# An adaLN transformer block on one core: the jump over the fallback program stands ahead of the last output transfers of SyncE and the last operations of VectorE

## The chip, the core and the metric

The kernel runs on one core of a Trainium2 chip. A core has five engines, each with its own instruction stream and its own sequencer: TensorE (PE in the profile, with PEld for its weight loads) multiplies matrices into PSUM, VectorE (DVE) and ScalarE (ACT) work element by element, GpSimd (POOL) does little here, and SyncE (SP) issues DMA transfers. Engines wait for each other through semaphores. The metric is the device time of the whole launch in microseconds (us), lower is better. Times of before and after are medians of several runs.

## The reference

One block with modulation from a condition `c`: six vectors (shift, scale and gate, for the attention and for the feed-forward half) come from `silu(c) @ w_mod`; then

```
h = layernorm(x) * (1 + ca) + sa
x = x + ga * attention(h)        # 32 query heads of 32, one key and value head, S = 2048
h = layernorm(x) * (1 + cb) + sb
x = x + gb * ((silu(h @ w1) * (h @ w3)) @ w2)     # D = 1024, F = 3584
```

All inputs and the output are bf16; `x` is 2048 x 1024. What matters for this case is the last line: for each group of rows, the product with `w2` is multiplied by the gate `gb`, added to `x`, and sent to the output in DRAM.

## The kernel before

The 2048 rows are worked on in 8 blocks of 256 rows (`NB`, `B`). For each block the attention, its output projection, the feed-forward's first half and its second half follow; blocks overlap, so that TensorE has products to do while ScalarE takes exponentials. The program is written as a graph of operations (`Graph.op`), and `Placer` puts them in an order, per engine, from a written list (`ORDER`). Each operation becomes a small function that issues its waits, its instruction and its semaphore update; `Placer.ops[name]` is the list of these functions for one engine. All of them are played through line 22, so line 22 is what the profile shows for nearly every instruction.

**Two programs.** The fast program takes the softmax without subtracting the row maximum. While it runs, VectorE checks that the sums stay in a safe range (`in_range`), and when the last block's sums are through, `verdict` writes one number, `AGAIN`: 0 if all was well. The same kernel holds a second, guarded program, in which the maximum is subtracted. Every engine first plays its whole list of the first program, then waits for the flag, loads `AGAIN` into a register (line 747), and compares and branches (line 748): if the number isn't 0 it plays the second program, otherwise it jumps over it. With the inputs here it is 0, so the second program is never run, but its instructions lie in each engine's stream between the first program and the end of the block. SyncE, after the jump, waits for the transfers of the first program's output (line 756). Line 758 is the end of the block, where the engines drain, meet at a barrier through GpSimd, and finish.

**The end of the first program.** The feed-forward's second half (`ffn2`, `quarter`, `result`) goes through four quarters of 256 output columns for a block. A quarter is 28 matmuls for each of two halves of 128 rows. For a whole quarter VectorE multiplies the 128x512 result by the gate (`HT<-S,GBR` in the profile) and adds it to `x` (`X<-X,HT`). In the last block each quarter is sent out as soon as it is summed, by a transfer of 128 KB on SyncE's queue; the last quarter is handled half by half, with 64 KB each. So the last things on VectorE are: product and sum of the third quarter, product and sum of the first half of the fourth, product and sum of its second half, six operations; and on SyncE the three transfers that belong to them. Each transfer has its own semaphore, for which line 756 waits.

Of the kernel before, what the change touches and what calls it, by code (L numbers as in the profile page):

```python
# [24 lines left out]
class Sess:  # L25
    __slots__ = ("bank", "nodes", "left", "prev", "strict", "allow", "fill")

    def __init__(self, strict=True):
        self.fill = False
        self.allow = ()  # L30
        self.strict = strict
        self.bank = None
        self.nodes = []
        self.left = 0
        self.prev = ()
# [375 lines left out]
class Placer:  # L411
# [6 lines left out]
    FULL = 36.0  # L418
    FETCH = 24.0
    GAP = 0.7  # L420

    def __init__(self, g, banks, later, plan, first=None, order=None):
        self.g = g
# [150 lines left out]
    def commit(self, n, e, k, start):  # L574
# [12 lines left out]
        if e == "pe" and self.warm and self.step == 0 and n.mode == "F":  # L587
            self.keep_warm(start)
        elif e == "pe" and self.warm and self.step and start - before > self.GAP:
            self.keep_on(before, start)  # L590
# [148 lines left out]
    def emit_all(self, second, flag, tile, outs):  # L739
        sem = self.sem  # L740
        last = self.finals()

        def both(eng, name):
            for fn in self.ops[name]:
                fn(eng)
            eng.wait_ge(sem[flag.sem], flag.val)
            again = eng.value_load(tile)
            with eng.If(again != 0):
                for s, v in last.items():
                    if v:  # L750
                        eng.wait_ge(sem[s], v)
                for fn in second.ops[name]:
                    fn(eng)
            if name == "sp":
                for n in outs:
                    eng.wait_ge(sem[n.sem], n.val)

        with self.nc.Block() as block:
            @block.gpsimd
            def _(e):  # L760
                both(e, "pool")

            @block.sync
            def _(e):
                both(e, "sp")

            @block.tensor
            def _(e):
                both(e, "pe")

            @block.scalar
            def _(e):
                both(e, "act")

            @block.vector
            def _(e):
                both(e, "dve")
# [892 lines left out]
```

## Time and profile before

| what | us |
|---|---|
| median of three runs | 1137.85 (1137.28 to 1138.27) |
| profiled execution | 1138.92 |
| its span, first to last instruction | 1137.1 |
| VectorE's last sum ends | 1132.50 |
| SyncE issues the output of the second quarter | 1120.70 |
| SyncE issues the last output | 1132.53 |

The span is what the trace's times refer to: 0 is its start. In the rows, an engine's name with a q behind it (SPq, DVEq, PEldq) means its sequencer, whose waits, loads of registers, branches and DMA issues aren't counted as busy time. A row of a group such as `x1: 505/505/505, 1132.9 to 1132.9` gives the least, median and greatest duration in nanoseconds, and then when the first and the last of the group start. In a timeline's row the first number is the start, the second the duration, and the bracket at its end the idle time ahead of it and what ended that. `q14 instruction` in a list of DMA queues is the fetching of instructions for an engine; `q1` carries the kernel's own transfers.

### The profile page before, as it was taken

The page shows a single profiled execution, that of the slowest core. Times are in us where ns is not written, and L with a number is a line of the kernel's source. Part 1 is how long each engine was busy: PE and PEld are TensorE (multiplying, and loading weights), DVE is VectorE, ACT ScalarE, POOL GpSimd, SP SyncE. Part 2 cuts the span into 40 slices and gives each one's busy share as a digit, 9 for nine tenths or more (in the row PEclk, how much of TensorE's full clock was granted, in tenths as well). Part 3 has the DMA queues.
Part 4 walks back from the last instruction along what each step waited for, and adds up shares of the span by engine and source line. Part 5 has one row for each costly group of instructions (what it writes and reads, how often), then busy time and mean ns, then how long its engine had stood idle before and what let it go on. Part 6 is the DMA issues. An engine that isn't in the chain of part 4 may idle for free.

```text
span 1137.1 us, 37432 instructions
## 1 busy us (share of the span) xinstructions
PE 1102.5 (97%) x16864; PEld 755.2 (66%) x16891; DVE 993.3 (87%) x1634; ACT 1020.4 (90%) x1159; POOL 42.9 (4%) x93
## 2 busy tenths in 40 slices
PE   5999989999899999999999999999999999999998
PEld 5744546766467766777577766776667757777887
DVE  7998999999999989998999889998999899997441
ACT  5999999999999999999999999999999999993110
POOL 5300000000100000000000000000000000000000
PEclk9999999999999999999999999999999999999999
DMA  9321477675656676865696568768587558767983
GB/s 344 107 76 36 146 212 203 191 203 144 174 150 192 183 188 157 240 195 152 122 297 193 151 179 209 223 193 214 149 249 214 161 141 214 214 188 195 260 233 85
DMA packets 381544, 209.73 MB, mean 184 GB/s; under 512 B 17600, under 2 KB 373184, under 8 KB 381376
## 3 DMA queue, kind: packets, MB, share of 16 engines
q1 hardware_dynamic: 380944, 207.11, 66.0%
q8 instruction: 135, 2.21, 0.8%
q14 instruction: 33, 0.27, 0.1%
q10 hardware_dynamic: 432, 0.13, 0.1%
HBM read 199.89 MB, written 4.19 MB: 179 GB/s over the span
## 4 chain that ended last, share of the span: by engine, by line
PE 47%; ACT 41%; DVE 6%; DMA 2%; POOL 1%; issue 1%; SPq 1%; DVEq 0%
ACT U L22 38%; PE PB L22 34%; PE S L22 13%; ACT HT L22 3%; DVE PS L22 2%; DMA W<-in_A_wq_dram 1%; DVE ST L22 1%; DVE HT L22 1%; POOL RS L22 1%; SPq L22 1%; DMA HT<-in_B_w_dram 1%; DVE QT L22 1%; DMA W<-in_B_w_dram 0%; DVE X L22 0%; DVE XNB L22 0%
## 5 line engine op out<-in xcount | busy, mean ns | idle before, releaser
L22 ACT ACTIVATE U<-S 128x1024 bf16<-128x1024 f32 x1024 | 967.0, 1141 | 6.2 <-PE S L22 5.0
L22 DVE TENSOR_TENSOR PS<-U 128x2048 bf16<-128x2048 bf16 x256 | 308.8, 1213 | 9.6 <-ACT U L22 8.1
L22 DVE TENSOR_TENSOR PS<-PS 128x1024 bf16<-128x1024 bf16 (+1 forms) x420 | 284.5, 690 | 4.2
L22 PE MATMUL PB<-QT,W 128*128 128x256 bf16 (+1 forms) x2632 | 223.5, 273 | 0.1
L22 PE MATMUL S<-QT,KT 32*128 32x256 bf16 x4096 | 203.9, 273 | 7.9 <-ACT U L22 5.3
L22 PEld LDWEIGHTS PB<-QT,W 128*128 128x128 bf16 (+1 forms) x2632 | 167.4, 97 | 40.8 <-issue 22.2
L22 PE MATMUL PB<-W2S,HT 128*128 128x256 bf16 x1512 | 189.6, 273 | 0.0
L22 PEld LDWEIGHTS PB<-W2S,HT 128*128 128x128 bf16 x1512 | 137.1, 98 | 41.6 <-issue 22.6
L22 PEld LDWEIGHTS S<-QT,KT 32*128 32x128 bf16 x4096 | 60.8, 92 | 135.4 <-ACT U L22 121.8
L22 PE MATMUL PB<-U,V 128*32 128x256 bf16 x4032 | 126.9, 273 | 0.8 <-ACT U L22 0.8
L22 PE MATMUL PB<-QT,HT 128*128 128x256 bf16 (+1 forms) x1288 | 123.9, 273 | 0.9 <-DVE QT L22 0.6
L22 PEld LDWEIGHTS PB<-U,V 128*32 128x32 bf16 x4032 | 99.4, 96 | 23.2 <-issue 13.5
L22 ACT ACTIVATE HT<-PB 128x512 bf16<-128x512 f32 (+1 forms) x110 | 81.6, 741 | 32.0 <-PE PB L22 31.9
L22 PEld LDWEIGHTS PB<-QT,HT 128*128 128x128 bf16 (+1 forms) x1288 | 90.9, 97 | 23.2 <-issue 11.5
L22 PE MATMUL PB<-HT,W 128*32 128x512 bf16 (+2 forms) x884 | 97.8, 342 | 2.8 <-DVE HT L22 0.9
L22 DVE SCALAR_TENSOR_TENSOR HT<-HT,PB 128x512 bf16<-128x512 bf16 x103 | 70.4, 684 | 12.7 <-ACT HT L22 11.8
L22 PEld LDWEIGHTS PB<-HT,W 128*128 128x128 bf16 (+1 forms) x896 | 50.4, 97 | 33.2 <-issue 11.7
L22 DVE TENSOR_TENSOR HT<-HT,PB 128x512 bf16<-128x512 bf16 x98 | 66.7, 681 | 1.3 <-PE PB L22 0.6
L22 PE MATMUL PB<-WO,QT 128*128 128x512 bf16 (+1 forms) x266 | 54.8, 380 | 1.6 <-issue 1.3
L22 DVE STREAM_TRANSPOSE RB<-PB 128x256 f32<-128x256 f32 x63 | 28.1, 446 | 29.2 <-PE PB L22 28.7
L22 POOL TENSOR_SCALAR RS<-MV 128x1 f32<-128x1 f32 x32 | 13.4, 418 | 1001.0 <-DVE MV L22 994.8
L22 ACT ACTIVATE HT<-S 128x512 bf16<-128x512 f32 (+1 forms) x13 | 9.4, 728 | 36.7 <-PE S L22 36.7
(122 smaller groups left out, 674.8 us busy)
## 6 DMA issues: line engine op xcount, KB each, us to landing
W<-in_B_w_dram SPq DMA_DIRECT2D x150, 512.0 KB, 4.9
W2S<-in_B_w_dram SPq DMA_DIRECT2D x30, 1792.0 KB, 9.3
HT<-in_B_w_dram SPq DMA_DIRECT2D x74, 512.0 KB, 5.0
W2S<-in_w_mod_dram SPq DMA_DIRECT2D x8, 1024.0 KB, 5.7
X<-in_A_x_dram SPq DMA_DIRECT2D x8, 512.0 KB, 6.7
U<-in_w_mod_dram SPq DMA_DIRECT2D x4, 1024.0 KB, 11.6
out_dram<-X SPq DMA_DIRECT2D x7, 512.0 KB, 8.1
W2S<-in_A_x_dram SPq DMA_DIRECT2D x5, 512.0 KB, 11.1
```

Source lines behind the costliest of these rows:

```text
L22: return getattr(e, call[0])(*call[1], **call[2])
```

## The change

`TAIL` names two engines and a number of list entries: 3 for SyncE, 6 for VectorE. These engines now play their list up to that tail, then wait for the flag, load `AGAIN` and branch. In the first `If` (the number isn't 0) the tail comes ahead of the second program, so that the first program is complete there too. A second `If`, on the same register being 0, stands behind it and plays the tail. Then the stream goes on as before: SyncE's waits for the outputs, and the end of the block. The other three engines have a tail of 0 and the same instructions as before. The tail is thus twice in the stream of each of the two engines, and played once.

```diff
+    TAIL = {"sp": 3, "dve": 6}
...
         def both(eng, name):
-            for fn in self.ops[name]:
+            ops = self.ops[name]
+            cut = len(ops) - self.TAIL.get(name, 0)
+            for fn in ops[:cut]:
                 fn(eng)
             eng.wait_ge(sem[flag.sem], flag.val)
             again = eng.value_load(tile)
             with eng.If(again != 0):
+                for fn in ops[cut:]:
+                    fn(eng)
                 for s, v in last.items():
                     if v:
                         eng.wait_ge(sem[s], v)
                 for fn in second.ops[name]:
                     fn(eng)
+            if ops[cut:]:
+                with eng.If(again == 0):
+                    for fn in ops[cut:]:
+                        fn(eng)
             if name == "sp":
                 for n in outs:
                     eng.wait_ge(sem[n.sem], n.val)
```

## The prediction

> **What bounds the kernel now.** I read the page's first lines, then the chain of waits over the last 45 us, because an edit at the end of two queues can touch nothing else, and then, line by line, what the sequencers do behind the last arithmetic. From the page, and from the chain between 1095 and 1140 us (start us, length us, what):
>
> ```profile
> span 1137.1 us, 37432 instructions
> PE 1102.5 (97%) x16864; PEld 755.2 (66%) x16891; DVE 993.3 (87%) x1634; ACT 1020.4 (90%) x1159; POOL 42.9 (4%) x93
> ```
>
> ```profile
> 1125.60 3.06 PE PB L22 x28
> 1128.66 3.07 PE S L22 x28
> 1131.73 0.02 issue
> 1131.75 0.44 DVE HT L22
> 1132.19 0.02 issue
> 1132.21 0.29 DVE X L22
> ```
>
> TensorE sets the pace until 1131.73, and the last operation of VectorE ends at 1132.21 + 0.29 = 1132.50. The span ends at 1137.1. So 4.6 us follow in which no engine computes, and the page counts none of it as busy. The groups of the three lines that run there (value load, branch, and the end of the block with line 756's waits; the times after the commas are first and last start) and SyncE's last issue in the timeline:
>
> ```profile
> L22 DVE TENSOR_SCALAR AGAIN<-S x1: 152/152/152, 1051.9 to 1051.9; 128x1 int32<-128x1 f32 x1
> L747 POOLq TENSOR_LOAD <-AGAIN x1: 498/498/498, 1052.1 to 1052.1; - x1
> L747 DVEq TENSOR_LOAD <-AGAIN x1: 544/544/544, 1132.2 to 1132.2; - x1
> L747 SPq TENSOR_LOAD <-AGAIN x1: 505/505/505, 1132.9 to 1132.9; - x1
> ```
>
> ```profile
> L748 POOLq COMPARE_BRANCH  x1: 45/45/45, 1052.6 to 1052.6; - x1
> L748 ACTq COMPARE_BRANCH  x1: 50/50/50, 1105.8 to 1105.8; - x1
> L748 PEldq COMPARE_BRANCH  x1: 3622/3622/3622, 1130.2 to 1130.2; - x1
> L748 DVEq COMPARE_BRANCH  x1: 72/72/72, 1132.8 to 1132.8; - x1
> L748 SPq COMPARE_BRANCH  x1: 53/53/53, 1133.5 to 1133.5; - x1
> ```
>
> ```profile
> L756 SPq EVENT_SEMAPHORE  x6: 17/28/28, 1136.3 to 1136.7; - x6
> ```
>
> ```profile
> L758 POOLq EVENT_SEMAPHORE  x2: 17/17/17, 1136.9 to 1137.0; - x2
> L758 POOLq DRAIN  x1: 107/107/107, 1053.1 to 1053.1; - x1
> L758 ACTq DRAIN  x1: 80/80/80, 1110.0 to 1110.0; - x1
> L758 PEldq DRAIN  x1: 73/73/73, 1133.8 to 1133.8; - x1
> L758 DVEq DRAIN  x1: 58/58/58, 1135.8 to 1135.8; - x1
> L758 SPq COMPARE_BRANCH  x1: 43/43/43, 1136.7 to 1136.7; - x1
> L758 SPq DRAIN  x1: 13/13/13, 1136.9 to 1136.9; - x1
> ```
>
> ```profile
> 1132.53 0.34 SPq L22 DMA_DIRECT2D out_dram<-X  x1
> ```
>
> Read them by engine. Each branch itself is shown as some 50 ns, but the next instruction of the engine comes much later: SyncE branches at 1133.5 and its first wait runs at 1136.3, **2.8 us** later; VectorE 1132.8 to its drain at 1135.8, 3.0; TensorE 3.6 (here the branch row itself is long); ScalarE 1105.8 to 1110.0, 4.2; GpSimd only 1052.6 to 1053.1, 0.5. GpSimd has by far the shortest program (x93 on the page). Instruction fetches have their own DMA rows, in three windows: around GpSimd's branch (1052 to 1054 us) none shows, around ScalarE's (1105.3 to 1110) one, behind the last arithmetic (1131.5 to 1138) four:
>
> ```profile
> q1 hardware_dynamic: 663, 0.34, 56.1%
> ```
>
> ```profile
> q1 hardware_dynamic: 1899, 0.97, 72.0%
> q14 instruction: 1, 0.01, 1.2%
> ```
>
> ```profile
> q14 instruction: 4, 0.03, 1.8%
> out_dram<-X SPq DMA_DIRECT2D x1, 64.0 KB, 1.6
> ```
>
> So I read the gap as the jump over a long second program to code that must be fetched. The same window gives the landing of the last transfer: 1.6 us after its issue at 1132.53, thus 1134.1. SyncE comes to its waits at 1136.3, when all transfers have landed for 2.2 us; the six waits then run through in 0.4. What ends last is SyncE's jump, not the output.
>
> **The change, part by part.**
>
> *SyncE's value load and branch move ahead of three issues.* The flag they wait for is written at 1051.9, so the wait costs nothing at either place. Today they stand behind the last issue, with nothing else in front of the end: from the issue's end (1132.53 + 0.34 = 1132.87) to the first wait, 3.4 us. Afterwards they follow the second quarter's output. SyncE's issues, and VectorE's operations in the same stretch:
>
> ```profile
> 1120.70 0.37 SPq L22 DMA_DIRECT2D out_dram<-X  x1
> ```
>
> ```profile
> 1126.82 0.37 SPq L22 DMA_DIRECT2D out_dram<-X  x1
> ```
>
> ```profile
> 1119.53 0.69 DVE L22 TENSOR_TENSOR HT<-S,GBR 128x512 bf16<-128x512 f32 x1 [4.96 <-PE S L22]
> 1120.25 0.42 DVE L22 TENSOR_TENSOR X<-X,HT 128x512 bf16<-128x512 bf16 x1
> 1125.64 0.69 DVE L22 TENSOR_TENSOR HT<-S,GBR 128x512 bf16<-128x512 f32 x1 [4.96 <-PE S L22]
> 1126.37 0.42 DVE L22 TENSOR_TENSOR X<-X,HT 128x512 bf16<-128x512 bf16 x1
> 1128.70 0.42 DVE L22 TENSOR_TENSOR HT<-PB,GBR 128x256 bf16<-128x256 f32 x1 [1.91 <-PE PB L22]
> ```
>
> The issue ends at 1121.07; with 0.5 for the load the branch stands at about 1121.65 and the next instruction at 1124.5 by SyncE's own 2.8, at 1125.9 by ScalarE's 4.2. The next issue is due at 1126.82, when its sum is ready. So SyncE's stall is covered by 0.9 to 2.3 us. Without that cover, the 128 KB output behind it would go out late by the excess; it has some 5.7 us before the last issue, so even that wouldn't reach the end. No queue but SyncE's own issues is passed.
>
> *VectorE's move ahead of six operations.* These are the product and the sum of the third quarter and of both halves of the fourth. The sequencer runs ahead of the engine (its load stands at 1132.2, the last sum's own start), so the load can start by 1120.3, the branch by 1120.9, and the next instruction comes at 1123.9 (by VectorE's 3.0) or 1125.1 (by 4.2). Its product is due at 1125.64, when TensorE is done with the quarter: cover 0.5 to 1.7 us. Were it late, the pair takes 1.15 us and the next product isn't due until 1128.70, 1.91 us of idle that absorb it. Behind the waiting VectorE stand only those outputs: the next 28 matmuls start at 1125.60, ahead of the product, so they don't wait for it, and the last 28 start 2.3 us after it ends. The profile shows no instruction fetch between 1120.6 and 1126 today, so the two new ones meet little traffic.
>
> *The second If.* Each of the two engines now compares once more, and falls through into its tail, and leaves it by a branch to what stands directly behind. No row shows such a jump on VectorE; the nearest are SyncE's jump from its last wait to the directly following drain (1136.7 to 1136.9, 0.2 us) and GpSimd's 0.5. The upper bound is the full 2.8. I take 0.2, since the target is adjacent. The compare lies under the same idle times; SyncE's exit runs from 1132.87 to 1133.1 under the last transfer's flight to 1134.1, with 1.0 us to spare. Cost nothing; with 2.8 it is the second rival below.
>
> *What ends last then.* SyncE waits for the last transfer: issue 1132.53, landing 1134.13. Its wait for that transfer stands sixth of line 756's six; from 1136.7, where that one runs, to the end of the span it is 0.4 us today (branch, drain, the barrier through GpSimd). New end 1134.13 + 0.4 = 1134.53, and 0.05 for a wake-up rather than a wait that is already met (the product above starts 0.02 to 0.04 behind its matmul): 1134.6. VectorE drains by 1132.7. **TensorE** is late next: it still branches at 1130.2 and drains at 1133.8 to 1133.9, 0.4 us ahead of SyncE's drain. Were its jump to take ScalarE's 4.2 instead of 3.6, it would drain at 1134.4 and cost 0.1. ScalarE and GpSimd are through long before.
>
> *Sum.* 1137.1 - 1134.6 = 2.5 us off the span. The profiled execution took 1138.92, 1.82 beyond its span and 1.07 above the median of the three runs; both stay as they are, so 1138.92 becomes 1136.4, and the median 1137.85 becomes **1135.35**.
>
> [...]
>
> **The rivals.**
>
> 1. *The forecast*, 1135.35; its own range goes from 1134.4 (0.4 more gain from spread between runs and 0.5 from a jump that costs more without the profiler, towards ScalarE's 4.2) to 1136.5 (landing 1.8 as for the 128 KB transfers, a slower TensorE jump, spread of 0.5 and a jump that costs less).
>
> 2. *The exit from the second If fetches too.* SyncE would jump at 1132.87 and come to its waits 2.8 later, at 1135.7; with the 0.8 from first wait to the end (1136.3 to 1137.1) that is 1136.5. Gain 0.6: 1137.25. For it: no row shows this jump. Against: the jump to the adjacent drain took 0.2.
>
> 3. *The stall isn't the jump's*, but that of something that ends at its own time, say a landing that the rows place wrongly; the jump itself is the 53 ns of its row. Then moving it changes nothing: 1137.85. Against: VectorE, which waits for no transfer there, shows the same gap.
>
> 4. *Slower: two fetches behind the last output.* If SyncE's tail and its waits come to lie in different pieces of fetched code, both the exit from the If and the jump from the last wait to the drain fetch. With J each, the end is 1132.87 + 2J + 0.8; from J = 1.7 on this is later than 1137.1. With 2.8 it is 1139.3, with 4.2 it is 1142.1; I take 3.2, near SyncE's and VectorE's: 1140.1, 3.0 more, 1140.85. For it: the tail shifts the code. Against: these are few instructions, and SyncE has from 1124.5 to 1132.5 to bring the next piece.
>
> **How the numbers follow.** Chances: forecast 0.83, second 0.07, third 0.04, fourth 0.06. The three others make 0.17, so the range is the forecast's own, rounded outward: 1134.3 to 1136.6. What a measurement here can tell from no change is about 0.2%, 2.28 us, thus 1135.57. The forecast lies only 0.22 below that, less than the 0.5 by which runs spread, and I give 0.68 of its 0.83 to faster; the other 0.15, with rivals two and three, make same 0.26; slower is rival four, 0.06.
>
> **What would show it.** In the profile after: SyncE's and VectorE's rows of the value load and the branch at about 1121, the last output issued still at 1132.5 and the product at 1125.6 (cover holds); line 756's last wait at 1134.1 rather than 1136.7; VectorE's drain below 1133, TensorE's at 1133.8; span 1134.6. A product later than 1125.7 would show the cover too short; first waits after 1135 the second or fourth rival; an unmoved end with an early branch the third. The prediction is wrong if the end follows anything but the landing.

## The result, and the profile after

| | before | after |
|---|---|---|
| median of 20 runs each, us | 1138.63 (1136.64 to 1140.70) | 1136.01 (1133.70 to 1138.29) |
| ratio, after to before | | 0.9976 (95%: 0.9969 to 0.9983) |
| profiled execution, us | 1138.92 | 1133.70 |
| its span | 1137.1 | 1131.9 |
| from the end of the last matmul to the end of the span | 5.42 | 2.85 |

The change makes the kernel 2.7 us faster (0.0024 x 1138.63; by the interval 1.9 to 3.5), where 2.5 was forecast. The two profiled executions differ by more, 5.2 us, and only half of that is the change's. The spread goes with the clock: of the 20 runs of after, the two fastest (1133.70, the profiled one, and 1134.30) had a mean granted clock of 1.000 and the two slowest (1138.29 and 1137.59) of 0.994; the profiled execution of before had 0.998. The chain of waits of the profile after (start us, length us, what):

```profile
1102.86 20.09 PE S L22 x184
1122.95 3.06 PE PB L22 x28
1126.01 3.07 PE S L22 x28
1129.08 0.02 issue
1129.10 0.44 DVE HT L22
1129.54 0.02 issue
1129.56 0.29 DVE X L22
```

It has the same pieces with the same lengths as before, but all of them 2.65 us earlier (1129.10 against 1131.75). That part isn't the change: nothing in the streams differs until the second quarter's output, and the whole of it is there 15 us ahead of that, where the first piece shown starts at 1102.86 (1105.51 in the chain before). The number that the branches test, written far ahead of any edited instruction, already stands 1.6 us earlier than before's 1051.9:

```profile
L22 DVE TENSOR_SCALAR AGAIN<-S x1: 152/152/152, 1050.3 to 1050.3; 128x1 int32<-128x1 f32 x1
```

Over the ten profiles of this study that write falls between 1050.3 and 1052.9, so this one is the earliest of a spread that each execution brings with it. What is to be compared is the piece behind the last matmul, which in the two profiles begins with the same 0.04 us, product and sum. From the end of the last sum (1129.85 here, 1132.50 before) to the end of the span it was 4.63 and is 2.06: **2.57 us**, by the trace's unrounded times. The groups by line of the profile after (new numbers: 750 the load, 751 the first branch, 760 the second If, 765 SyncE's waits for the outputs, 767 the end):

```profile
L751 DVEq COMPARE_BRANCH  x1: 72/72/72, 1118.2 to 1118.2; - x1
L751 SPq COMPARE_BRANCH  x1: 58/58/58, 1119.0 to 1119.0; - x1
L751 PEldq COMPARE_BRANCH  x1: 3448/3448/3448, 1127.5 to 1127.5; - x1
```

```profile
L760 DVEq COMPARE_BRANCH  x1: 50/50/50, 1121.2 to 1121.2; - x1
L760 SPq COMPARE_BRANCH  x1: 40/40/40, 1121.6 to 1121.6; - x1
```

```profile
L765 SPq EVENT_SEMAPHORE  x6: 17/28/28, 1130.3 to 1131.5; - x6
```

```profile
L767 POOLq EVENT_SEMAPHORE  x2: 17/17/17, 1131.7 to 1131.8; - x2
...
L767 DVEq DRAIN  x1: 330/330/330, 1129.6 to 1129.6; - x1
L767 PEldq DRAIN  x1: 73/73/73, 1131.0 to 1131.0; - x1
L767 SPq COMPARE_BRANCH  x1: 38/38/38, 1131.5 to 1131.5; - x1
L767 SPq DRAIN  x1: 13/13/13, 1131.7 to 1131.7; - x1
```

Compare line 765 with line 756 of before. There, the first wait came long after everything had landed, and six waits ran through in 0.4 us. Now the first runs at 1130.3, directly behind the issue of the last transfer, and the last at 1131.5, because it truly waits. In the timeline, that issue; in the DMA view of 1129.8 to 1132, its landing 1.6 us later, at 1131.4 to 1131.5; and VectorE's product behind its early branch:

```profile
1129.88 0.34 SPq L22 DMA_DIRECT2D out_dram<-X  x1
```

```profile
out_dram<-X SPq DMA_DIRECT2D x1, 64.0 KB, 1.6
```

```profile
1122.99 0.69 DVE L22 TENSOR_TENSOR HT<-S,GBR 128x512 bf16<-128x512 f32 x1 [4.96 <-PE S L22]
```

VectorE's idle time ahead of that product is 4.96 us, to the hundredth what it was, though it now holds a load, a branch and a fetch. The four fetches that the window behind the last arithmetic had before now stand between 1118 and 1123 (0.03 MB in four packets, 8 KB each), and that queue has none from 1129.8 on:

```profile
q14 instruction: 4, 0.03, 1.9%
```

### The profile page after: what moved, and what is told of

Its sections match the earlier page's. It is cut to its first block, busy times and chain, and to the rows that moved or that the text cites. A ratio compares the mean times of both kernels' runs of the same rounds, so it can differ in the third digit from the quotient of the medians.

```text
span 1131.9 us, 37461 instructions
## 1 busy us (share of the span) xinstructions
PE 1104.5 (98%) x16891; PEld 755.2 (67%) x16891; DVE 993.4 (88%) x1634; ACT 1019.9 (90%) x1159; POOL 43.1 (4%) x93
## 3 DMA queue, kind: packets, MB, share of 16 engines
q8 instruction: 135, 2.21, 0.8%
## 4 chain that ended last, share of the span: by engine, by line
PE 47%; ACT 43%; DVE 5%; DMA 2%; POOL 1%; issue 1%; SPq 1%; DVEq 0%
ACT U L22 40%; PE PB L22 34%; PE S L22 13%; ACT HT L22 3%; DVE PS L22 2%; DMA W<-in_A_wq_dram 1%; DVE HT L22 1%; POOL RS L22 1%; SPq L22 1%; DVE ST L22 1%; DMA HT<-in_B_w_dram 1%; DVE X L22 0%; DVE QT L22 0%; DVE RB L22 0%; POOL WO L22 0%
## 5 line engine op out<-in xcount | busy, mean ns | idle before, releaser
L22 PE MATMUL PB<-HT,W 128*32 128x512 bf16 (+2 forms) x896 | 100.1, 342 | 1.2 <-DVE HT L22 0.9
L22 PE MATMUL PB<-WO,QT 128*128 128x512 bf16 (+1 forms) x280 | 57.8, 380 | 0.0
```

Of the source, the lines that this page charges most:

```text
L22: return getattr(e, call[0])(*call[1], **call[2])
```

## The experiments

Eight kernels, each profiled once. Whole times of single executions spread by 4 us, so what follows rests on the stretch behind VectorE's third-quarter product or behind the last matmul. The latter is 2.85 to 2.87 in the change and in the three kernels of these that end as it does.

**1. SyncE's move alone, and VectorE's move alone.**

```diff
-    TAIL = {"sp": 3, "dve": 6}
+    TAIL = {"sp": 3}
```

> Only SyncE's three transfers stand behind the branch, VectorE branches after its last sum as before. Measured from the end of TensorE's last matmul to the end of the span: 5.4 us before, 2.8 after the change. My theory: VectorE's jump (its drain comes 3.3 after its last sum ends) is what ends last now, so about 4.3. Rival (the gain is SyncE's alone, VectorE's move does nothing): 2.8.

```diff
-    TAIL = {"sp": 3, "dve": 6}
+    TAIL = {"dve": 6}
```

> Only VectorE's six operations stand behind the branch, SyncE branches after its last transfer as before. My theory: SyncE's jump still ends last, 5.4 from the last matmul to the end, no gain. Rival (each move brings its share): between 2.8 and 5.4, some 4.

Measured from the last matmul to the end: 4.30 with SyncE's move alone, 5.14 with VectorE's alone. The rows by line with SyncE's alone:

```profile
L751 DVEq COMPARE_BRANCH  x1: 72/72/72, 1130.6 to 1130.6; - x1
```

```profile
L767 SPq DRAIN  x1: 13/13/13, 1132.2 to 1132.2; - x1
L767 DVEq DRAIN  x1: 58/58/58, 1133.5 to 1133.5; - x1
```

SyncE is done at 1132.2, and the barrier waits for VectorE until 1133.5: its branch at 1130.6 and 2.9 us from there to its drain. With VectorE's move alone it is the other way round:

```profile
L751 SPq COMPARE_BRANCH  x1: 53/53/53, 1133.0 to 1133.0; - x1
```

```profile
L767 DVEq DRAIN  x1: 330/330/330, 1131.7 to 1131.7; - x1
L767 PEldq DRAIN  x1: 73/73/73, 1133.5 to 1133.5; - x1
...
L767 SPq DRAIN  x1: 12/12/12, 1136.1 to 1136.1; - x1
```

VectorE's move by itself brings nearly nothing, yet with SyncE's it brings the second 1.45 us (4.30 to 2.85). The 0.3 that it does bring alone, where none was expected, is SyncE's jump at 2.6 instead of 2.8. That VectorE's fetch is out of its way doesn't explain it: in experiment 3 VectorE fetches nothing beside it (from 1132.5 to the end that queue has one fetch of 8 KB, at about 1135.8, behind SyncE's branch at 1134.6) and SyncE's jump takes 2.8. Over the eight profiles with a far jump on SyncE it takes 2.5 to 2.9, so the 0.3 lies within the spread. Both rivals fall: with SyncE's move alone the end isn't at 2.8, and with VectorE's alone it isn't at some 4.

**2. A short second program, branches where they were.** Edit of the kernel before; the second program, which isn't run with these inputs, is left out on the two engines but for its first 20 entries:

```diff
-                for fn in second.ops[name]:
+                short = 20 if name in ("sp", "dve") else None
+                for fn in second.ops[name][:short]:
                     fn(eng)
```

> The branches stand where they stood before the change, but the second program is left out on SyncE and VectorE except for its first 20 list entries (it isn't run with these inputs), so the jump is short. My theory (the gap is the fetch of far code): the next instruction comes 0.2 to 0.5 after the branch instead of 2.8 and 3.0, SyncE is at its waits before the landing, and the end comes 2.8 after the last matmul, as with the change. Rival (a branch taken costs 2.8 wherever it goes): 5.4.

Measured: 3.06. The rows of line 748, of SyncE's waits (line 757 here), and of the end:

```profile
L748 DVEq COMPARE_BRANCH  x1: 72/72/72, 1133.2 to 1133.2; - x1
L748 SPq COMPARE_BRANCH  x1: 58/58/58, 1133.9 to 1133.9; - x1
```

```profile
L757 SPq EVENT_SEMAPHORE  x6: 17/28/28, 1134.4 to 1134.7; - x6
```

```profile
L759 DVEq DRAIN  x1: 17/17/17, 1133.4 to 1133.4; - x1
```

From branch to next instruction SyncE takes 0.5 and VectorE 0.2, where they took 2.8 and 3.0. So the same branch, taken the same way, lost its stall here when the target was near: what these two engines paid for is the distance, not the branch. Between 1133.2 and 1134.8 the DMA rows of this run show no instruction fetch, where before had two of 8 KB from 1132.6 to 1135. It stays 0.2 above the change because load, jump and six waits still run one after another behind the last issue, from 1133.3 to 1134.7, and end later than the landing (about 1134.5, estimated: the issue stands 0.4 ahead of the load, as in the kernel before, and lands 1.6 later).

**3. How far is near?** The same edit with 170 entries kept on SyncE (a jump over 195 instructions) and 20 on VectorE.

```diff
-                for fn in second.ops[name]:
+                short = {"sp": 170, "dve": 20}.get(name)
+                for fn in second.ops[name][:short]:
                     fn(eng)
```

> As the run with a short second program, but 170 list entries of it stay on SyncE (195 instructions to jump over, where 45 took 0.5 us and 341 took 2.8), and 20 on VectorE. [...]

```profile
L748 SPq COMPARE_BRANCH  x1: 53/53/53, 1134.6 to 1134.6; - x1
```

```profile
L757 SPq EVENT_SEMAPHORE  x6: 17/28/28, 1137.4 to 1137.7; - x6
```

2.8 us again, 5.36 from the last matmul to the end. So a jump over 45 instructions (SyncE) or 113 (GpSimd, 0.5) is near, and one over 195 isn't. SyncE's second program has 341 instructions in the kernel before; these counts are of the programs as built, not of a trace. Where between, and whether it depends on the place within a fetched piece, wasn't tried.

**4. Later places for the branches.** One operation pair and one transfer later, and two:

```diff
-    TAIL = {"sp": 3, "dve": 6}
+    TAIL = {"sp": 2, "dve": 4}
```

> The branches stand ahead of SyncE's last two transfers and VectorE's last four operations. Measured from the start of VectorE's third-quarter product to the end of the span: 11.5 us before, 8.9 after the change. My theory: VectorE comes back 3.0 after a branch that stands 1.3 after that product's start, so the next product runs some 1.2 late, but the 2.3 us of idle ahead of the last product absorb it: 8.9. Rival (the lateness is passed on to the last transfer): about 10.1.

```diff
-    TAIL = {"sp": 3, "dve": 6}
+    TAIL = {"sp": 1, "dve": 2}
```

> The branches stand later: ahead of SyncE's last transfer and VectorE's last product and sum. My theory (the stall is hidden only as far as the idle time reaches): VectorE branches 0.6 after the first half's sum is issued and comes back 3.0 later, 1.0 after its last product is due; the end is 3.8 after the last matmul. Rival (any place ahead of the end serves): 2.8.

Measured: 8.95 (the change: 8.93) for the first, 3.82 from the last matmul for the second. VectorE's timeline of the first, then of the second:

```profile
1126.03 0.69 DVE L22 TENSOR_TENSOR HT<-S,GBR 128x512 bf16<-128x512 f32 x1 [4.96 <-PE S L22]
...
1130.50 0.42 DVE L22 TENSOR_TENSOR HT<-PB,GBR 128x256 bf16<-128x256 f32 x1 [3.32 <-PE S L22]
1130.96 0.29 DVE L22 TENSOR_TENSOR X<-X,HT 128x256 bf16<-128x256 bf16 x1
1132.14 0.42 DVE L22 TENSOR_TENSOR HT<-S,GBR 128x256 bf16<-128x256 f32 x1 [0.89 <-PE S L22]
```

```profile
1130.05 0.29 DVE L22 TENSOR_TENSOR X<-X,HT 128x256 bf16<-128x256 bf16 x1
1133.60 0.43 DVE L22 TENSOR_TENSOR HT<-S,GBR 128x256 bf16<-128x256 f32 x1 [3.25 <-PE S L22]
```

In the first, the middle product stands 4.47 after the one before it instead of 3.06, 1.4 late (1.2 was expected), its idle time has grown from 1.91 to 3.32, and the next idle time has shrunk from 2.31 to 0.89 by the same 1.4. The last product is on time. In the second nothing is left to shrink: the last product is 0.95 late, and the end with it. A third place would have to be still earlier, and the change's own shows by 1.8 us of spare time on VectorE that earlier brings nothing.

**5. TensorE too.**

```diff
-    TAIL = {"sp": 3, "dve": 6}
+    TAIL = {"sp": 3, "dve": 6, "pe": 14}
```

> As the change, and TensorE branches too, ahead of its last 14 list entries, the last 28 matmuls. My theory (a stall is hidden only where the engine idles, and TensorE doesn't): its sequencer runs 2.1 us ahead of its matmuls, load and branch take 4.0 to 4.6, so it stands idle some 2.2 us and the end comes at 11.1 after the third product's start. Rival (its queue covers the jump): 8.9, with TensorE's drain 1.9 us earlier than after the change.

Measured: 14.68, 5.75 later than the change where 2.2 was expected; whole time 1142.04 against 1138.18 for a single run of the kernel before beside it. TensorE's timeline and a table by stretches (us from to, length, then busy time of each engine with its count, granted clock, DMA share, GB/s):

```profile
1130.77 1.15 PE L22 MATMUL S<-U,HT 128*128 128x256 bf16 x9 [2.18 <-issue]
1133.82 3.58 PE L22 MATMUL S<-U,HT 128*128 128x256 bf16 x19 [1.90 <-issue]
```

```profile
1128.60:1130.70 2.10, 0.00 (x0) 0.00 (x0) 0.71 (x2) 0.00 (x0) 0.00 (x0) 1.00 0.11 31
1130.70:1132.00 1.30, 1.15 (x9) 0.90 (x10) 0.00 (x0) 0.00 (x0) 0.00 (x0) 1.00 0.05 13
1132.00:1133.80 1.80, 0.00 (x0) 0.00 (x0) 0.00 (x0) 0.00 (x0) 0.00 (x0) 0.83 0.00 0
1133.80:1136.00 2.20, 2.18 (x11) 1.52 (x11) 0.00 (x0) 0.00 (x0) 0.00 (x0) 0.50 0.00 0
1136.00:1137.40 1.40, 1.39 (x10) 0.87 (x8) 0.00 (x0) 0.00 (x0) 0.00 (x0) 0.79 0.00 0
```

The first idle time is the 2.2 of the theory. Then come two things that it didn't have. After nine matmuls the engine stands again for 1.9, waiting for nothing that the profile shows. TensorE's fetches are 16 KB (q8 on the page of the kernel before: 135 packets, 2.21 MB), and the table shows where they can be. From 1128.60 to 1130.70 it has 31 GB/s for 2.10 us, 65 KB, which the first half's output of 64 KB fills. From 1130.70 to 1132.00, behind the engine's second branch at 1130.6, it has 13 GB/s for 1.30 us, 17 KB, about one such fetch, and from 1132.00 to 1133.80 nothing. So in this run the code of the nine matmuls was on its way before 1128.60, and the following piece not until the first one ran. That is the mechanism of the prediction's fourth rival, on another engine. And the granted clock falls to 0.50 behind these idle times: eleven matmuls begin in 2.2 us, 0.2 us for one, where one takes 0.11 at a clock of 1.00. Counted from start to start, beyond the usual 0.11, the first gap is 2.3 (1128.31 to 1130.77) and the second 2.1 (1131.65 to 1133.82; both first starts reckoned from the 0.109 us between matmuls). The 19 matmuls behind them take 1.3 longer (3.30 from the first's start to the last's, against 18 times 0.109 = 1.97). Together that makes 5.7.

**6. No branch at all.** No engine waits for the flag, loads or branches, and the second program is left out.

```diff
-            eng.wait_ge(sem[flag.sem], flag.val)
-            again = eng.value_load(tile)
-            with eng.If(again != 0):
...
```

> No engine waits for the flag, loads it or branches, and the second program is left out. My theory (the change hides all that the jump cost): 8.9 after the third product's start, as after the change, with the landing of the last transfer ahead of the end. Rival (part of the jump or of the second If is still in the path): clearly less than 8.9, by up to the 0.4 between the landing and the end.

Measured: 8.92 after the third product's start, 2.85 from the last matmul, as with the change. So nothing of the jump is left in the path, and no better place for it is to be found: to shorten the end, the last product, sum and transfer would have to be shortened.

## Why the prediction was right

- *The end is SyncE's jump, and the jump is a fetch.* Shown: shortening what is jumped over removes the stall (2.8 to 0.5) with the branch in its place; 195 instructions bring it back (2.8). So the stall of these two engines hangs on where the target lies. Their fetches are 8 KB each (four packets, 0.03 MB).
- *The third rival*, that something else ends there at its own time, is out: the end moved with the branch. The second, an exit from the second If that fetches, didn't occur: SyncE's first wait comes at 1130.3, 0.06 after the end of its last issue (1129.88 + 0.34 = 1130.22), so this exit costs less than the 0.2 taken. The fourth didn't occur on SyncE or VectorE; on TensorE its mechanism did (the second gap of 1.9 in experiment 5).
- *The cover.* VectorE was back at 1121.2 with its product due at 1122.95, 1.8 to spare (1.7 by its own fetch); SyncE at 1121.6 with its next issue at 1124.16, 2.5 to spare (2.3), since its fetch took 2.6 instead of 2.8. That lateness is absorbed by the idle time behind it, and how far, is the pair of runs in experiment 4.
- *What ends last then.* The landing, as forecast: issue to landing 1.6, the last wait to the end 0.46 (0.4 and 0.05 forecast). TensorE is next: it drains at 1131.0, 0.6 ahead of SyncE's drain (0.4 forecast).
- *Both moves are needed*, which the prediction's sum had in it (VectorE's drain at 1135.8 would have ended last) but didn't say: alone, SyncE's gives 1.1 of the 2.57, VectorE's 0.3, no more than the spread of SyncE's jump.
- *The size.* 2.57 in the span's tail against 2.5 forecast. The time, 1136.01, is 0.66 above the 1135.35 forecast, because the three runs of before that it was reckoned from (1137.85) lie 0.8 under the median of 20. The spread of runs, put at 0.5, is some 2 to each side. The forecast gave 0.68 to a gain beyond 2.28, the least that it thought could be told from none; the measured 2.7, with its interval of 1.9 to 3.5, doesn't settle on which side of 2.28 the gain lies. With runs that spread by 2 and a forecast only 0.22 beyond that bound, the chance should have been nearer to even. That the time still lies in the range of 1134.3 to 1136.6 is in part luck: the base was off by more than the 0.5 that the range allowed for spread.

## What to carry to other kernels

A jump over a long block of code cost 2.5 to 4.3 us here, on each of the four engines with a long second program. Only on TensorE does the branch's own row show it (3.4 to 4.0 us, where the others' first branches show 45 to 72 ns), so look at when the engine's next instruction runs. Put such a jump where that engine idles for longer, ahead of the last work that waits for others, and move it on every engine whose jump ends behind the new end, for moving one of two brings only the difference to the second (here 1.1 and 0.3 of the 2.57). Don't move it on the engine that sets the pace: there the part of load and jump that the sequencer's lead doesn't cover (2.2 of 4.2 us in experiment 5) is paid, and so is what follows from the idle time.

## What the runs showed beside it

In experiment 5 the idle TensorE cost more than its idle time: after two gaps of 2.2 and 1.9 us the clock was granted at half (0.50 from 1133.80 to 1136.00), and that added some 1.3 us to 19 matmuls. Whether one such gap would have done it wasn't tried.

A fetch beside an output in flight: the second quarter's output landed 2.7 us after its issue with the change, 2.9 with VectorE's move alone and 2.8 in experiment 5, against 1.8 in the kernel before, with SyncE's move alone and without branches. The three late ones are those in which VectorE branches about when this transfer is issued, 0.2 behind it (1118.0 and 1118.2 with the change, 1120.2 and 1120.4, 1120.6 and 1120.8). In the first kernel of experiment 4 an output of 64 KB, issued at 1131.28, was late too, with no branch of VectorE beside it (that stands at 1127.3; TensorE's is at 1130.5):

```profile
out_dram<-X SPq DMA_DIRECT2D x1, 64.0 KB, 2.7
```

It cost nothing in any of these runs, since the last output landed later still. Nor is a branch of VectorE beside a transfer enough: in the kernel before, its fetch starts at 1133.83, while the last output is in flight, and that output landed in the usual 1.6. Which overlap makes a transfer late isn't shown.
